# Six moves in a fused strided-attention and MLP kernel: a load, a memset, the order of a sum, two matmuls, four attention pieces and a store

## The chip, the cores and the metric

The kernel runs on one core of a Trainium2 chip. The metric is the device time of one execution in microseconds (us), as the median of several runs. Beside it stands one execution that was recorded by the hardware profiler; its rows give start and duration of each instruction, counted from the start of the recorded span.

## The reference

There are 8 batches of 8 heads, with 576 positions and a head dimension of 64. Heads 0 to 3 attend to the last 32 positions, heads 4 to 7 to all earlier positions with the same remainder modulo 32. The attention's output, 4608 tokens of 512 numbers, goes through a two-layer MLP with a PReLU between the layers.

```python
mask_local = (rel >= 0) & (rel < stride)
mask_strided = (rel >= 0) & (pos[None, :] % stride == pos[:, None] % stride)
masks = np.stack([mask_local if h < H // 2 else mask_strided for h in range(H)], axis=0)
scores = np.where(masks[None, :, :, :], scores, -1000000000.0)
...
attn = attn / (np.sum(attn, axis=-1, keepdims=True) + 1e-09)
...
h = x @ w_in
g = np.maximum(h, 0.0) + alpha * np.minimum(h, 0.0)
return (g @ w_out).astype(np.float32)
```

Inputs and outputs are float32; the kernel works in float16 with float32 accumulation. w_in is 512x2048, w_out 2048x512.

## The kernel before

**Attention** goes by pairs of heads. Pair g belongs to batch g // 4; the first two pairs of a batch are local (6 blocks of 96 queries against 128 keys), the last two strided (8 residues with 72 queries and keys). For each pair there are pieces: T turns q or k of the local heads by TensorE, S (`score_both`, or `sc1` in the part written by hand) computes scores, exponentiates them on ScalarE (ACT) and multiplies them by a mask on GpSimd (POOL) or VectorE (DVE), P (`pv_piece`) multiplies by v and divides by the sum of the row, which is a reciprocal (L437) and a multiplication (L439) on DVE, and X turns the result into `xT`, the MLP's input with tokens along the free axis. From batch 2 on, most turns are DMA transposes on SyncE's (SP's) queue: `x_dma` for the result, `transpose_d` for the strided q and k. These are first loaded row by row into `qsd` and `ksd` by `load_d(b)`, two DMAs on POOL's queue; there is one such buffer for each of q and k, so a batch's load waits until the transposes of the batch before have read it. P28.1 means the second P piece of pair 28.

**The MLP** goes by 9 chunks of 512 tokens. The first layer of chunk n is 16 pieces (`lin1_piece(n, m)`), each with four 128x512 matmuls over kk, the four pairs of heads in `xT` (L613). Each writes a PSUM bank `hps`, of which there are three. ACT makes `neg`, the negated negative part (L621), and DVE joins both to `gT` (L624) and frees the bank. The second layer of chunk 0 is plain: `U(kf)` (L884) does three token tiles and `W(i)` (L899) two matmuls of the fourth, with kf = 2i and 2i + 1. From chunk 1 on the second layer is a 2x2x2 product with seven multiplications in place of eight (`lin2_fast`, steps "1" to "7"), which needs sums of the weights (`wsum`, made once) and of the activations (`gsum`, L653, made for each chunk on POOL and DVE). A step stores its 256x256 block by `store` (L664 on DVE where something is added, L662 on ACT otherwise), followed by a DMA on SP's queue.

**Order.** Every instruction is wrapped in `keep`, so each engine runs its instructions in the order in which the program emits them. The start and chunk 0's second layer are lists written by hand. For chunks 1 to 8 there is a loop of 30 steps: step i is a first-layer piece for i < 16 and a part of the second layer after that, and behind each step a number of attention pieces (`cnt`) is emitted. For most chunks that number comes from a running sum, half as fast in the first 16 steps as later; chunk 6 has a list of steps of its own. `late` holds functions that are called at the start of the next `attn_step`; with `cnt` at 0, `attn_n` still calls `attn_step` once, which empties the list.

```python
for nm in "qk":
    keep(nc.vector.memset(qks[nm][64:80], 0.0))
keep(nc.vector.memset(x16s[64:80], 0.0))
keep(nc.vector.tensor_copy(id32, ident[0:72, 0:72]))
...
keep(nc.gpsimd.memset(vss[0][:, :, :, 64:65], 1.0))
...
load_v(0, True)
load_v(0, False)
for c in range(4):
    load_w(c, False)
```

`x16s` is the result buffer of the strided pairs from batch 2 on; its rows 72 to 79 are padding that the DMA transposes read. `load_v(0, True)` loads `stv` (the strided v), `load_v(0, False)` loads `vl` (the local v), `load_w` the parts of w_in; all are on POOL's queue.

Of the kernel before, what the change touches and what calls it, by code (L numbers as in the profile page):

```python
# [9 lines left out]
F32 = mybir.dt.float32  # L10
F16 = mybir.dt.float16
ALU = mybir.AluOpType
# [20 lines left out]
def kernel(  # L33
# [10 lines left out]
    nc = tc.nc  # L44
# [421 lines left out]
    def x_dma(P):  # L466
        if P.strided:
            P.xs = xpool.tile([128, 8, 80], F16, tag="xs", bufs=2, name="xs")
            keep(nc.sync.dma_start_transpose(P.xs, P.x16[0:80, :]))
        else:  # L470
            for s0, d0, w in spans(P.b):
                keep(nc.sync.dma_start_transpose(
                    xT[:, P.hp, d0 : d0 + w].rearrange("r (w p) -> r w p", p=96),
                    P.x16[0:96, 128 * (s0 // 96) : 128 * ((s0 + w) // 96)]))
# [14 lines left out]
    def T(u, nm):  # L489
        return lambda: transpose_piece(u, nm)  # L490
# [10 lines left out]
    for g in range(7, npair + 2):  # L501
        c = g // 4
        a, p, t = g, g - 1, g + 1
        okA = 8 <= a < npair
        okP = 8 <= p < npair
        okT = 8 <= t < npair and t < 4 * NX and (t % 4 == 0 or t < 4 * DX and t % 2 == 0)
        nP = len(pairs[p].pgroups) if okP else 0
        seq = []
        if okA:
            seq.append(("S", lambda a=a: score_both(pairs[a])))  # L510
        if okP:
            seq.append(("P", Pv(p, 0)))
        if okT:
            seq.append(("T", T(t // 2, "q")))
        if 8 <= g - 2 < npair and not pairs[g - 2].xd:
            seq.append(("X", X(g - 2)))
        if okP:
            seq.append(("P", Pv(p, 1)))
        if okT:
            seq.append(("Tk", T(t // 2, "k")))  # L520
        if nP == 3:
            seq.append(("P", Pv(p, 2)))
        if g == 14:
            seq[0], seq[1] = seq[1], seq[0]
        if not seq:
            seq.append(("N", lambda: None))

        todo = [(c, pr) for pr in range(2)] if g % 4 == 0 and 8 < g < npair else []

        if g % 4 == 1 and 9 <= g and c + 1 < B:  # L530
            todo = [(c + 1, nm) for nm in "qk"]
        lastP = max([i for i, z in enumerate(seq) if z[0] == "P"], default=len(seq) - 1)
        nslots = [i for i, z in enumerate(seq) if z[0][0] != "S"] or list(range(len(seq)))
        for i, (kind, fn) in enumerate(seq):
            extra = []
            if todo and i in nslots:
                left = len([z for z in nslots if z >= i])
                cnt = -(-len(todo) // max(1, left))
                extra = [todo.pop(0) for _ in range(min(cnt, len(todo)))]

            def run(fn=fn, extra=extra, g=g, c=c, kind=kind, lastp=(i == lastP), first=(i == 0),
                    second=(i == min(1, len(seq) - 1))):
                fn()
                for b, pr in extra:
                    if pr in ("q", "k"):
                        if b == 3:
                            continue
                        if b < NX:
                            cast_l(b, pr)
                        if b + 1 < NX:  # L550
                            load_qk(b + 1, pr)
                        continue
                    if b == 3:
                        continue
                    cast_v(b, pr, "pool")
                    if pr == 1 and b + 1 < B:
                        load_v(b + 1, True)
                if first and g % 4 == 2 and NX <= c + 1 < B:
                    turn_rows(c + 1)
                if lastp and g % 4 == 3 and NX <= c + 2 < B:  # L560
                    load_rows(c + 2, "k")
                if lastp:
                    if 4 * DX <= g - 1 < npair and pairs[g - 1].xd:
                        x_dma(pairs[g - 1])
                    if g % 4 == 3 and DX < c + 1 < B:
                        transpose_d()
                    if g % 4 == 2 and DX < c and c + 1 < B:
                        load_d(c + 1)
                    if g % 4 == 1 and DX < c and c + 1 < B:
                        load_v(c + 1, False)  # L570
                    if g % 4 == 1 and NX <= c + 2 < B:
                        load_rows(c + 2, "q")
                if second and 4 * DX <= g - 3 < npair and pairs[g - 3].xd and pairs[g - 3].strided:
                    after.append(lambda: x_copy(pairs[g - 3]))
            feed(run, g - 2 if kind == "X" else -1)
# [25 lines left out]
    def lin1_piece(n, m, begin=False):  # L601
        if n not in gTs:
            gTs[n] = gpool.tile([128, 16, 512], F16, tag="gT", name="gT")
        c0 = (512 * n) % RING
        hps = begun.pop(m, None)
        if hps is None:
            pool, tag = (pspool, "ps") if n == 0 and m // 3 % 2 else (phpool, "hps")
            hps = pool.tile([128, 512], F32, tag=tag, name="hps")
            order = (0, 1, 2, 3) if n else (2, 3, 0, 1)
        else:  # L610
            order = (0, 1)
        for kk in order[0:2] if begin else order:
            keep(nc.tensor.matmul(  # L613
                hps, win16[:, kk, 128 * m : 128 * m + 128], xT[:, kk, c0 : c0 + 512],
                start=(kk == (0 if n else 2)), stop=(kk == (3 if n else 1))))
        if begin:
            begun[m] = hps
            return

        neg = npool.tile([128, 512], F32, tag="neg", name="neg")  # L620
        keep(nc.scalar.activation(neg, hps, AF.Relu, scale=-1.0))  # L621

        def fin():
            keep(nc.vector.scalar_tensor_tensor(  # L624
                gTs[n][:, m, :], neg, oma[:, m : m + 1], hps, op0=ALU.mult, op1=ALU.add))
        late.append(fin)
# [43 lines left out]
    bank = {}  # L670

    def lin2_fast(n, i):
# [58 lines left out]
        if x == "1":  # L731
            bank["b"] = phpool.tile([128, 512], F32, tag="hps", name="ops")
            keep(nc.scalar.copy(bank["b"], bank["a"]))
        elif x in "56":
            z = npool.tile([128, 512], F32, tag="par", bufs=2, name="par")
            keep(nc.scalar.copy(z, bank[b]))  # L736
            bank["s" + x] = z
        elif x == "2":
            store(n, 0, 0, bank["a"])
        elif x == "7":  # L740
            late.append(lambda: store(n, 1, 1, bank["b"], bank["s5"]))
        elif x == "3":
            late.append(lambda: store(n, 0, 1, bank["e"], bank["s6"]))
        else:
            store(n, 1, 0, bank["b"])
# [40 lines left out]
    keep(nc.vector.memset(kTs[0][:, :, 608:672], 0.0))  # L786
    for nm in "qk":
        keep(nc.vector.memset(qks[nm][64:80], 0.0))
    keep(nc.vector.memset(x16s[64:80], 0.0))
    keep(nc.vector.tensor_copy(id32, ident[0:72, 0:72]))  # L790

    keep(nc.gpsimd.memset(vss[0][:, :, :, 64:65], 1.0))
# [30 lines left out]
    def ov(b, eng, c0, c1):  # L823
        return lambda: over_v(b, eng, c0, c1)
# [82 lines left out]
    def ws(z):  # L907
        return lambda: wout_sum(z, "dve", 0)

    def sc1(g, eng="dve"):  # L910
        return lambda: score_both(pairs[g], eng)

    for fn in [
        vs(1, 0, "pool"), sc1(6), U(0), vs(1, 1, "pool"), U(1), sc1(7), U(2), U(3), Cl(1, "q", "act"), Pv(6, 1),
        Cl(1, "k"), Pv(6, 2), Pv(6, 0), U(4), U(5), Pv(7, 0), Pv(7, 1), U(6), loads2, T(2, "q"), U(7), Pv(7, 2), W(0), W(1),
        T(2, "k"), ws(0), ws(1), ws(2), W(2), sc1(4), U(8), W(3), ov(1, "dve", 0, 24), U(9), sc1(5, "pool"), W(4), U(10), X(7, "act"), U(11),
        X(6, "act"), Pv(4, 1), W(5), Cl(2, "q", "act"), Cl(2, "k", "act"), U(12), Pv(4, 0), U(13), Pv(5, 0), U(14), Pv(5, 1),
        U(15), W(6), X(4, "dve"), X(5, "dve"), W(7)]:
        fn()
# [18 lines left out]
    for n in range(1, NCH):  # L938
# [3 lines left out]
        for i in range(30):  # L942
# [5 lines left out]
            if n == 1 and i == 15:  # L948
                held.extend(late)
                late.clear()  # L950
            if n == 6:
                cnt = int(i in (2, 5, 7, 9, 16, 17, 19, 20, 22, 24, 25, 27))
            elif n == 1:
                cnt = int(i > 12 or i in (0, 2, 4, 6, 9, 11))
            else:
                acc += left / (19.5 if n == B - 2 else 21) * (0.5 if i < 16 else 1.0)
                cnt = int(acc)
                acc -= cnt
# [14 lines left out]
                load_v(3, True)  # L973
            if i == 15:
                load_v(3, False)
                load_d(3)
                cast_l(3, "q", "act")
            if i == 17:
                cast_l(3, "k", "act")
# [35 lines left out]
```

## Time and profile before

| | |
|---|---|
| median of 3 runs | 297.91 us (297.36 to 298.34) |
| profiled execution, its own time | 296.76 us |
| its span | 294.9 us |
| granted TensorE clock | 1.0 |
| PE busy | 289.3 us |
| DVE, ACT, POOL busy | 216.1, 182.1, 181.7 us |
| DMA engines | busy for most of the first 28 of 40 slices, little after |

The span is what the recorded instructions cover; the rest of the profiled execution's time lies around it. Busy time of PE counts matmuls in flight, so a high share says that PE is rarely without work, not that it works at its peak. PE, PEld (the weight loads beside it), DVE, ACT, POOL and SP are the engines; an "issue" in place of a releaser means that the profile shows nothing that the engine waited for.

### The profile page before, as it was taken

The numbers are of one execution on the slowest core, as the hardware profiler recorded it, in microseconds if no ns is written. First come the engines' busy times: TensorE is split into PE (matmuls) and PEld (weight loads), VectorE is DVE, ScalarE is ACT, GpSimd is POOL, SyncE is SP. The second block draws the span as 40 slices with busy tenths as digits, with TensorE's granted clock in tenths as the row PEclk, the third lists the DMA queues.
The fourth block names the chain that finished last, engine by engine and source line by source line (L and its number), as shares of the span: only waits on it lengthen the run. The fifth ranks groups of instructions, "written<-read, shape, count | busy, mean of one in ns | idle before, by whom it ended". The sixth has DMA issues, their size and how long they took to land.

```text
span 294.9 us, 6948 instructions
## 1 busy us (share of the span) xinstructions
PE 289.3 (98%) x2732; PEld 187.3 (64%) x2732; DVE 216.1 (73%) x412; ACT 182.1 (62%) x337; POOL 181.7 (62%) x167
## 2 busy tenths in 40 slices
PE   8999999999999999999999999999999999999995
PEld 3764554545885488547864786478646864784584
DVE  5688876579966895689668975897489948927851
ACT  1777756797957864775477537754776266417630
POOL 8462547999589997889897985777364105002200
PEclk9999999999999999999999999999999999999999
DMA  7999999999999999999999999976411230021004
GB/s 180 263 194 203 239 212 258 221 158 336 114 110 196 153 151 129 195 136 153 174 185 146 122 144 194 134 115 117 150 20 23 58 109 0 0 87 58 2 0 143
DMA packets 97488, 41.18 MB, mean 140 GB/s; under 512 B 75360, under 2 KB 94256, under 8 KB 97456
## 3 DMA queue, kind: packets, MB, share of 16 engines
q0 software_dynamic: 51008, 17.77, 59.7%
q1 hardware_dynamic: 46096, 22.32, 37.2%
q10 hardware_dynamic: 352, 0.66, 0.9%
q8 instruction: 21, 0.34, 0.5%
q14 instruction: 11, 0.09, 0.1%
HBM read 38.24 MB, written 9.44 MB: 162 GB/s over the span
## 4 chain that ended last, share of the span: by engine, by line
PE 91%; DVE 3%; DMA 2%; issue 2%; ACT 1%; SPq 0%; DVEq 0%; ACTq 0%
PE hps L613 41%; PE ops L719 22%; PE ops L709 8%; PE pv L430 5%; PE ops L884 4%; PE sp L377 2%; DMA consts<-consts 2%; PE tp L292 1%; PE xp L455 1%; PE sph L377 1%; PE ops L899 1%; DVE gT L624 1%; PE tf L154 1%; DVE gsum L653 1%; PE wps L761 1%
## 5 line engine op out<-in xcount | busy, mean ns | idle before, releaser
L613 PE MATMUL hps<-xT,win 128*128 128x512 f16 x576 | 132.9, 379 | 0.1
L624 DVE SCALAR_TENSOR_TENSOR gT<-neg,oma,hps 128x512 f16<-128x512 f32 x144 | 105.2, 744 | 36.2 <-ACT neg L621 28.6
L621 ACT ACTIVATE neg<-hps 128x512 f32<-128x512 f32 x144 | 85.8, 598 | 34.6 <-PE hps L613 32.4
L613 PEld LDWEIGHTS <-win 128*128 128x128 f16 x576 | 53.3, 98 | 58.3 <-issue 0.8
L653 POOL TENSOR_TENSOR gsum<-gT 128x1024 f16<-128x1024 f16 x15 | 31.8, 2123 | 37.6 <-DVE gT L624 37.5
L402 POOL TENSOR_TENSOR et<-et,consts 128x576 f16<-128x576 f16 (+1 forms) x23 | 32.1, 1394 | 34.7 <-ACT et L400 34.4
L719 PEld LDWEIGHTS <-gT 128*128 128x128 f16 x384 | 35.7, 98 | 6.1 <-issue 0.5
L439 DVE TENSOR_TENSOR x<-pv,rc 96x384 f16<-96x384 f32 (+2 forms) x62 | 33.0, 532 | 2.1
L719 PE MATMUL ops<-wout,gT 128*128 128x256 f16 x256 | 32.1, 273 | 0.0
L709 PE MATMUL ops<-wsum,gsum 128*128 128x256 f16 x248 | 30.7, 273 | 0.2 <-DVE gsum L653 0.2
L409 POOL TENSOR_TENSOR et<-et,consts 128x576 f16<-128x576 f16 (+1 forms) x23 | 29.7, 1290 | 0.1
L430 PEld LDWEIGHTS <-et 72*128 72x128 f16 (+1 forms) x448 | 23.6, 98 | 8.4 <-ACT et L339 0.4
L709 PEld LDWEIGHTS <-gsum 128*128 128x128 f16 x256 | 23.6, 98 | 3.3 <-DVE gsum L653 0.4
L719 PEld LDWEIGHTS <-gsum 128*128 128x128 f16 x256 | 23.7, 98 | 2.9
L400 ACT ACTIVATE et<-sp 128x576 f16<-128x576 f32 (+1 forms) x24 | 15.5, 645 | 16.4 <-PE sp L377 16.4
L664 DVE TENSOR_TENSOR osb<-ops,par 128x512 f32<-128x512 f32 (+1 forms) x16 | 10.7, 674 | 17.1 <-PE ops L719 9.4
L437 DVE RECIPROCAL rc<-pv 72x6 f32<-72x6 f32 (+2 forms) x80 | 14.7, 183 | 10.2 <-PE pv L430 9.8
L662 ACT COPY osb<-ops 128x512 f32<-128x512 f32 x16 | 9.4, 587 | 16.8 <-PE ops L719 16.7
L406 ACT ACTIVATE et<-sph 128x288 f16<-128x288 f32 (+1 forms) x48 | 18.9, 409 | 0.0
L736 ACT COPY par<-ops 128x512 f32<-128x512 f32 x15 | 8.8, 587 | 13.1 <-PE ops L709 12.6
L719 PE MATMUL ops<-wsum,gT 128*128 128x256 f16 x128 | 16.1, 273 | 0.3 <-DVE osb L664 0.3
L719 PE MATMUL ops<-wsum,gsum 128*128 128x256 f16 x128 | 16.1, 272 | 0.0
(112 smaller groups left out, 354.5 us busy)
## 6 DMA issues: line engine op xcount, KB each, us to landing
out_dram<-osb SPq DMA_DIRECT2D x35, 256.0 KB, 3.0
vl<-in_v_dram POOLq DMA_DIRECT2D x6, 384.0 KB, 9.7
win<-in_moe_w_in_dram POOLq DMA_DIRECT2D x4, 512.0 KB, 17.4
wout<-in_moe_w_out_dram POOLq DMA_DIRECT2D x4, 512.0 KB, 17.1
qsd<-in_q_dram POOLq DMA_DIRECT2D x7, 288.0 KB, 7.5
ksd<-in_k_dram POOLq DMA_DIRECT2D x7, 288.0 KB, 8.8
stv<-in_v_dram POOLq DMA_DIRECT2D x7, 288.0 KB, 7.7
ql<-in_q_dram SPq DMA_DIRECT2D x3, 576.0 KB, 8.8
```

The costliest lines, as they stand in the source:

```text
L400: keep(nc.scalar.activation(ev.rearrange("r (y c) -> r y c", y=2), sp[0:r, :, 0:n], AF.Exp, scale=SCALE))
L402: keep(mul(mv, mv, m, op=ALU.mult))
L406: keep(nc.scalar.activation(ev[:, n * y : n * y + n], sps[y][0:r, 0:n], AF.Exp, scale=SCALE))
L409: keep(mul(mv, mv, m, op=ALU.mult))
L430: keep(nc.tensor.matmul(pv[:, 65 * x : 65 * x + 65], et[0:r, c : c + 128], v16[0:r, 2 * P.pr + hh, t, :] if P.strided else v16[:, 6 * (2 * ...
L439: keep(nc.vector.tensor_tensor(P.x16[0:w, c0 : c0 + 64 * nb].rearrange("r (c e) -> r c e", e=64), pvv[:, :, 0:64], rc[0:w, 0:nb].unsqueeze ...
L613: keep(nc.tensor.matmul(hps, win16[:, kk, 128 * m : 128 * m + 128], xT[:, kk, c0 : c0 + 512], start=(kk == (0 if n else 2)), stop=(kk == ( ...
L621: keep(nc.scalar.activation(neg, hps, AF.Relu, scale=-1.0))
L624: keep(nc.vector.scalar_tensor_tensor(gTs[n][:, m, :], neg, oma[:, m : m + 1], hps, op0=ALU.mult, op1=ALU.add))
L653: keep((nc.vector if eng == "dve" else nc.gpsimd).tensor_tensor(gsum[i][:, hs], a, b, op=op))
L709: keep(nc.tensor.matmul(o, gsum[i][:, y, 128 * z : 128 * z + 128], wsum[i][:, y, :], start=(x == "5" and y == 0 and (z == 0 or alone)), st ...
L719: keep(nc.tensor.matmul(o, lhs(y), rhs(y), start=(first and y == 0), stop=(y == 7), skip_group_check=True))
```

## The change

There are six edits. `load_d(3)` leaves step 15 of chunk 1 and stands in the piece after which `x_dma(pairs[10])` is emitted. The memset of `x16s` goes from DVE to POOL. In chunk 1, the first layer runs over kk in the order 2, 3, 0, 1, as chunk 0 does. In chunk 0's second layer, `W(3)` goes ahead of the scores of pair 4 and `U(8)`. Chunk 6 loses its own list of steps and follows the running sum. In the last chunk, step "7" adds in two halves and stores at once, not by `late`.

```diff
                     if 4 * DX <= g - 1 < npair and pairs[g - 1].xd:
                         x_dma(pairs[g - 1])
+                    if g == 11:
+                        load_d(3)
                     if g % 4 == 3 and DX < c + 1 < B:
                         transpose_d()
...
-            order = (0, 1, 2, 3) if n else (2, 3, 0, 1)
+            order = (0, 1, 2, 3) if n > 1 else (2, 3, 0, 1)
...
-                start=(kk == (0 if n else 2)), stop=(kk == (3 if n else 1))))
+                start=(kk == (0 if n > 1 else 2)), stop=(kk == (3 if n > 1 else 1))))
...
+        elif x == "7" and last:
+            osb = opool.tile([128, 512], F32, tag="osb", name="osb")
+            for z in range(2):
+                c = slice(256 * z, 256 * z + 256)
+                keep(nc.vector.tensor_tensor(osb[:, c], bank["b"][:, c], bank["s5"][:, c], op=ALU.add))
+            keep(nc.sync.dma_start(
+                out[512 * n + 256 : 512 * n + 512, 256:512].rearrange("(r p) c -> p r c", p=128),
+                osb.rearrange("p (r c) -> p r c", r=2)))
         elif x == "7":
             late.append(lambda: store(n, 1, 1, bank["b"], bank["s5"]))
...
-    keep(nc.vector.memset(x16s[64:80], 0.0))
+    keep(nc.gpsimd.memset(x16s[64:80], 0.0))
...
-        T(2, "k"), ws(0), ws(1), ws(2), W(2), sc1(4), U(8), W(3), ov(1, "dve", 0, 24), U(9), sc1(5, "pool"), W(4), U(10), X(7, "act"), U(11),
+        T(2, "k"), ws(0), ws(1), ws(2), W(2), W(3), sc1(4), U(8), ov(1, "dve", 0, 24), U(9), sc1(5, "pool"), W(4), U(10), X(7, "act"), U(11),
...
-            if n == 6:
-                cnt = int(i in (2, 5, 7, 9, 16, 17, 19, 20, 22, 24, 25, 27))
-            elif n == 1:
+            if n == 1:
                 cnt = int(i > 12 or i in (0, 2, 4, 6, 9, 11))
             else:
                 acc += left / (19.5 if n == B - 2 else 21) * (0.5 if i < 16 else 1.0)
...
             if i == 15:
                 load_v(3, False)
-                load_d(3)
                 cast_l(3, "q", "act")
```

## The prediction, made before the changed kernel had run

> **What bounds the kernel now.** I read the page's busy times first, then its chain, then the timeline in the five stretches that the diff touches.
>
> ```profile
> PE 289.3 (98%) x2732; PEld 187.3 (64%) x2732; DVE 216.1 (73%) x412; ACT 182.1 (62%) x337; POOL 181.7 (62%) x167
> PE 91%; DVE 3%; DMA 2%; issue 2%; ACT 1%; SPq 0%; DVEq 0%; ACTq 0%
> ```
>
> PE is busy for 98% of the span and carries 91% of the chain, at full granted clock. A 128x512 matmul costs 0.216 us (the chain's stretch at 239.20: 13.81 us for 64). No edit adds or removes a matmul, so only PE's few waits can move. These are the ones near the edits, from the timeline (start, duration, engine, line, operation; in brackets the idle time before it and who ended it):
>
> ```profile
> 1.41 1.55 POOL L212 DMA_DIRECT2D stv<-in_v_dram  x2 [0.25 <-issue]
> 4.49 0.48 DVE L789 MEMSET x16s<- 16x512 uint32 x1
> 6.89 0.19 DVE L790 CAST id<-consts 72x72 f32<-72x72 f16 x1 [1.92 <-DMA consts<-consts]
> 10.12 0.43 DVE L232 COPY vs<-stv 72x1024 f16<-72x1024 f16 x1 [0.32 <-DMA stv<-in_v_dram]
> 11.20 0.35 PE L430 MATMUL pv<-vs,et 72*128 72x65 f16 x6
> ...
> 44.39 0.59 PE L899 MATMUL ops<-wout,gT 128*128 128x512 f16 x2
> 44.59 0.72 DVE L232 COPY kT<-tp 128x512 f16<-128x512 f16 x1 [0.73 <-PE tp L292]
> 45.46 0.30 PE L377 MATMUL sp<-qT,kT 64*128 64x96 f16 x6 [0.47 <-DVE kT L232]
> 46.48 0.59 PE L899 MATMUL ops<-wout,gT 128*128 128x512 f16 x2
> ...
> 220.83 0.55 DVE L439 TENSOR_TENSOR x<-pv,rc 96x384 f16<-96x384 f32 x1
> 221.30 2.20 DVE L624 SCALAR_TENSOR_TENSOR gT<-neg,oma,hps 128x512 f16<-128x512 f32 x3
> 222.09 2.25 PEld L613 LDWEIGHTS <-win 128*128 128x128 f16 x11 [0.40 <-issue]
> 226.90 1.76 DVE L653 TENSOR_TENSOR gsum<-gsum,gT 128x1024 f16<-128x1024 f16 x1
> 230.41 1.05 PE L709 MATMUL ops<-wsum,gsum 128*128 128x256 f16 x8 [0.23 <-DVE gsum L653]
> ...
> 288.23 1.02 DVE L664 TENSOR_TENSOR osb<-ops,par 128x512 f32<-128x512 f32 x2 [4.03 <-issue]
> 288.98 1.91 PE L719 MATMUL ops<-wsum,gT 128*128 128x256 f16 x16 [0.32 <-DVE osb L664]
> ```
>
> Read each group as: what arrives last before PE goes on. At 10.12 it is the strided v (stv); at 45.46 the copy of batch 1's k; at 222.09 a DVE that is behind; at 230.41 a DVE sum; at 288.98 a DVE store.
>
> **The named edit, load_d(3): nothing.** In the program it moves from step 15 of chunk 1 into the piece P10.2 at step 21. The order of instructions on each engine shows what that does. On POOL's queue the two loads stand where they stood, between the load of vl and the mask of pair 12's scores, because between steps 15 and 21 POOL is given nothing (pair 11's masks are DVE's, and the q and k casts go to ACT). Both wait for the same semaphores at the same values. On SP nothing moves: its transposes of pair 10's x, then of qsd and ksd, keep their order and waits. An identical queue has an identical cost, 0.
>
> **Memset of x16s, from DVE to POOL: +0.2.** DVE is freed of the 0.48 at 4.49, but it then idles 1.92 for the constants, so that gains nothing. On POOL it becomes the first instruction, ahead of every POOL load, and the memset of vs behind it now waits for its end. It writes 1024 f16 elements per row. The nearest rows bound its time: POOL's memset of 32x64 took 0.22, its copies of 72x1024 f16 at 33.08 took 2.02 for two. I take 1.0, from the row with the same count. [...]
>
> So the issues of stv, vl and win slip by about 1.0. If stv lands 1.0 later, DVE's copy ends at 11.55, the first PV matmul starts at about 11.65 in place of 11.20, and DVE's cast of qT, which stands behind that copy and opens the scores of pair 3, ends near 12.0 in place of 11.11: PE resumes at 12.05 in place of 11.47, 0.6 late. PE, ACT and DVE then follow each other up to chunk 0, so the 0.6 stays. The cover is queueing. The two 144 KB stv loads land 8.7 after issue, later ones of 288 KB in 7.7 (median), with the DMA engines at 7 and 9 tenths in the first slices: part of the 8.7 is not the issue's. A third of 0.6 is my value, 0.2; the ends are -0.3 (stv earlier by DVE's 0.32 of idle time) and +1.05 (below).
>
> **W(3) ahead of sc1(4): -0.43.** W(2)'s second matmul has handed over at 44.39 + 2 x 0.216 = 44.82; PE then waits until 45.46, 0.64. W(3)'s two matmuls (those at 46.48) need only gT 6 and 7 and wout, both long there: 2 x 0.216 = 0.43 of the wait is filled. Scores 4 still start at 45.46, and U(9) and all behind it come 0.43 sooner. What could be late next: scores 5 at 47.65 would come at 47.22, with their two PSUM banks free when the exps at 46.34 (0.71) end, at 47.05. PV 4 at 50.27 needs masks that end at 47.95. Covered. The whole wait would be -0.64, half the fill -0.2.
>
> **Order of kk in chunk 1: 0.** The first piece reads pairs 6 and 7 first, so X(4) and X(5) have 0.43 more. The weight load there waited 0.35 for DVE, but PE only 0.03 behind W(7). It guards the 0.43 of the edit before, whose DVE work at this place may not come earlier in full.
>
> **Chunk 6's spread: -0.28.** The formula gives the steps 3, 6, 9, 12 in place of 2, 5, 7, 9; the eight from 16 on stay. A lin1 piece costs PE 0.863 and DVE 0.66 back to back; a PV adds 0.19 to PE and 0.69 to DVE. Before, P29.0 and P29.1 stand two pieces apart, DVE gains 2 x 0.20 between them and falls behind: gT of step 10 ends at 222.04, and the matmul of step 13, which needs its bank, starts at 222.09 instead of 221.81: 0.28. With steps 9 and 12, counted from the chunk's first matmul: step 13 can start at 12.25 and gT 10 ends at 12.23, a tie; gT 12 ends at 13.65 before step 15 at 13.97; gT 15 starts when its neg is there. So PE reaches step 16 0.28 sooner, DVE too. POOL's first sum now stands ahead of pair 30's mask and starts at about 5.1, since its four gT are done; pair 30's masks then end by 10.2, PV 30 wants them after 15. The wait of 0.23 at 230.41 comes from DVE's sum of 1.76 (others 0.69) beside POOL's mask of pair 31, which keeps its step, so it stays. Ends: -0.5 (that wait goes as well) and +0.2 (the tie is lost, or the sums start late).
>
> **Last chunk's "7": +0.07.** The store leaves `late`, but that list was emptied right after the same step, so its place is the same. What changes is one add of 512 (0.69) into two of 256, each 0.42 (row at 291.85); they overlap by 0.08, as the two adds at 288.23 do: 0.34 + 0.42 = 0.76. Only the second half signals, and the matmul at 288.98 waits for that: +0.07, straight to the end. Ends 0 and +0.1.
>
> **Sum:** 0 + 0.2 - 0.43 + 0 - 0.28 + 0.07 = -0.44. The profiled execution took 296.76 (span 294.9, 1.9 around it), which is 1.15 under the median of the runs, 297.91. It becomes 296.3; the median 297.5.
>
> **The rivals.**
>
> *POOL's loads come sooner.* [...] Chance 0.3, with both of its sizes.
>
> *The memset holds win too (slower).* The first part of win is waited for by POOL's wout issue at 19.71, the first lin1 matmul is at 19.64: no slack. If the slip of 1.0 reaches win whole, PE stands at that matmul, 1.05 late: 1.05 - 0.43 - 0.28 + 0.07 = +0.41, 298.3. It decides above a slip of 0.64. Against it: win lands 15 to 21 after issue, with the DMA engines full, and full engines make up a late issue. Chance 0.15.
>
> *Chunk 6 loses.* PV 29 at step 12 is nearer to the sums at 16. If DVE enters them late, +0.2 for -0.28: +0.04, 298.0; no change. Chance 0.1.
>
> **From cases to numbers.** The forecast has 0.45. A measurement here tells some 0.3%, 0.9 us (the three runs lie 0.98 apart). Over 0.9 faster: most of the first rival and a part of the forecast's spread, 0.36; slower by that: a part of the second rival with an unfavourable draw of runs, 0.15; between, 0.49. The range takes the first rival's larger size (296.6) and the second's end (298.3) with a little of the runs' scatter: 296.5 to 298.5.
>
> **What would show it.** Right: POOL's first load near 2.4 and stv's copy on DVE at 10.1 to 10.5; four L899 matmuls in a row ahead of scores 4; no gap at step 13 of chunk 6; two adds of 0.42 near 288; POOL's qsd and ksd loads at their old place. Wrong: the first lin1 matmul a whole microsecond late, a wait at 45 as long as before, or a wait for DVE sums in chunk 6 above 0.4.

## The result, and the profile after

The changed kernel takes 296.51 us (median of 21 runs, 295.54 to 301.99); the kernel before, beside it, 297.36 (21 runs, 296.45 to 298.87). The ratio is 0.9966 (95% interval 0.9955 to 0.9977): 1.0 us less, between 0.7 and 1.3 (the two medians lie 0.85 apart). The prediction had 0.44 less.

The profiled execution of the changed kernel is not a typical one: 297.44 us with a span of 295.6, so 0.7 longer than the profiled execution of before (296.76), though the median is shorter. What follows is therefore read stretch by stretch. First two lines of its page: the busy times, and the shares of the chain that ended last.

```profile
PE 289.3 (98%) x2732; PEld 187.5 (63%) x2732; DVE 215.7 (73%) x412; ACT 182.2 (62%) x337; POOL 183.4 (62%) x168
PE 67%; DMA 21%; DVE 4%; POOL 2%; ACT 2%; issue 2%; SPq 0%; POOLq 0%; DVEq 0%; ACTq 0%
```

PE's work is the same 289.3 us. But in this execution the chain runs through DMAs for 21% of the span (2% before): loads landed late. The timeline of the changed kernel at the five places shown of before, and at a sixth (88 to 91 us); start, duration, engine, line, operation, and in brackets the idle time before it and who ended it:

```profile
0.73 0.94 POOL L799 MEMSET x16s<- 16x1024 f16 x1 [0.29 <-POOLq L1006]
1.95 1.56 POOL L212 DMA_DIRECT2D stv<-in_v_dram  x2
10.51 0.43 DVE L232 COPY vs<-stv 72x1024 f16<-72x1024 f16 x1 [0.66 <-DMA stv<-in_v_dram]
11.24 0.35 PE L430 MATMUL pv<-vs,et 72*128 72x65 f16 x6
...
44.43 1.03 PE L909 MATMUL ops<-wout,gT 128*128 128x512 f16 x4
45.51 0.30 PE L377 MATMUL sp<-qT,kT 64*128 64x96 f16 x6
...
54.20 1.15 ACT L230 CAST kl<-kl 128x1152 f16<-128x1152 f32 x1 [1.13 <-DMA kl<-in_k_dram]
55.26 1.07 ACT L230 COPY osb<-ops 128x512 f32<-128x512 f32 x2
55.89 1.02 PE L615 MATMUL hps<-xT,win 128*128 128x512 f16 x4 [0.50 <-ACT osb L230]
...
89.03 1.40 ACT L478 COPY xT<-xs 128x384 f16<-128x384 f16 x2 [1.30 <-DMA xs<-x16s]
90.85 2.10 PE L615 MATMUL hps<-xT,win 128*128 128x512 f16 x9 [0.46 <-ACT xT L230]
...
223.18 2.75 PE L615 MATMUL hps<-xT,win 128*128 128x512 f16 x12
224.74 0.55 DVE L439 TENSOR_TENSOR x<-pv,rc 96x384 f16<-96x384 f32 x1
225.21 2.21 DVE L626 SCALAR_TENSOR_TENSOR gT<-neg,oma,hps 128x512 f16<-128x512 f32 x3
226.00 1.03 PE L721 MATMUL ops<-wout,gT 128*128 128x256 f16 x8
226.00 0.75 PEld L721 LDWEIGHTS <-gT 128*128 128x128 f16 x7 [0.34 <-issue]
228.06 0.69 DVE L655 TENSOR_TENSOR gsum<-gsum,gT 128x1024 f16<-128x1024 f16 x1
228.09 1.79 POOL L402 TENSOR_TENSOR et<-et,consts 72x576 f16<-72x576 f16 x1 [4.90 <-ACT et L400]
228.40 1.91 PE L711 MATMUL ops<-wsum,gsum 128*128 128x256 f16 x16
230.33 1.04 PE L711 MATMUL ops<-wsum,gsum 128*128 128x256 f16 x8
...
288.80 0.81 DVE L746 TENSOR_TENSOR osb<-ops,par 128x256 f32<-128x256 f32 x2 [3.68 <-issue]
289.61 0.42 DVE L666 TENSOR_TENSOR osb<-ops,par 128x256 f32<-128x256 f32 x1
289.66 1.91 PE L721 MATMUL ops<-wsum,gT 128*128 128x256 f16 x16
```

What to see: POOL's memset takes 0.94 and its first load is issued at 1.95 (before 1.41), and DVE's copy of stv starts at 10.51 (before 10.12), when stv lands; the first PV matmul is 0.04 later than before. Four matmuls stand ahead of scores 4. At 55.89 PE waits for ScalarE, which had waited for k. At 89.03 ScalarE waits 1.30 for pair 10's turned x, and PE for ScalarE. In chunk 6 no wait is left at step 13, but one of 0.34 for the weights (0.23 for PE) has come up at 226.00, where the second layer begins. The row names no releaser, but the semaphores of the trace do: step 16 writes the PSUM bank of step 13, which DVE frees with the gT of step 13, the first of the three at 225.21. DVE makes it after the PV of step 12 (224.74) and signals its end at 225.96, and PE goes on 0.04 later. The DVE sum that took 1.76 beside POOL's mask now takes 0.69, and the matmuls at 228.40 and 230.33 follow without a wait. At 288.80 the first half of the add comes 3.68 after DVE's last work; before, it was 4.03.

The runs scatter, so I cut each profile into stretches between the first matmuls of its parts. The same stretch has the same length in all kernels unless something in it differs. The runs of e1 to e4, e5 to e8, e9 to e12 and e13 to e16 were taken on four chips, each with the kernel before beside them (medians 297.34, 297.33, 297.31 and 297.47), so compare ratios, not medians. In us:

| kernel | first PV to first lin1 | layer 2 of chunk 0, to chunk 1 | chunk 1 | chunk 2 | chunk 6 | chunk 8 to last matmul | median | ratio to before (95%) |
|---|---|---|---|---|---|---|---|---|
| before | 8.44 | 19.64 | 33.38 | 30.94 | 29.49 | 26.41 | 297.36 | |
| after | 8.44 | 20.05 | 33.61 | 31.63 | 29.03 | 26.18 | 296.51 | 0.9966 (0.9955 to 0.9977) |
| e1: store alone | 9.20 | 19.64 | 33.38 | 30.97 | 29.49 | 26.47 | 297.48 | 1.001 (0.9989 to 1.003) |
| e2: chunk 6 alone | 8.44 | 19.64 | 33.38 | 30.96 | 29.03 | 26.41 | 296.98 | 0.9992 (0.9974 to 1.0009) |
| e3: W(3) and kk alone | 8.44 | 19.19 | 33.23 | 31.42 | 29.49 | 26.43 | 296.77 | 0.9989 (0.997 to 1.0008) |
| e4: named load alone | 8.45 | 19.64 | 33.38 | 31.31 | 29.48 | 26.41 | 297.53 | 1.0001 (0.9983 to 1.0019) |
| e5: memset alone | 8.44 | 19.64 | 33.38 | 30.96 | 29.49 | 26.06 | 296.91 | 0.9977 (0.9956 to 0.9999) |
| e6: after without memset | 8.87 | 19.19 | 33.24 | 32.11 | 29.03 | 26.47 | 296.8 | 0.9981 (0.996 to 1.0002) |
| e7: after without store | 8.44 | 19.67 | 33.23 | 30.98 | 29.03 | 26.05 | 295.9 | 0.9944 (0.9926 to 0.9962) |
| e8: after again | 8.44 | 19.19 | 33.64 | 32.64 | 29.03 | 26.19 | 296.7 | 0.9971 (0.995 to 0.9992) |
| e9: e7, load behind | 8.44 | 19.19 | 33.23 | 31.44 | 29.03 | 26.05 | 296.34 | 0.9968 (0.9957 to 0.998) |
| e10: load behind alone | 8.74 | 19.97 | 33.73 | 31.44 | 29.49 | 26.43 | 297.55 | 1.001 (0.9998 to 1.0022) |
| e11: W(3) alone | 8.70 | 19.21 | 33.38 | 30.93 | 29.49 | 26.41 | 296.94 | 1.0 (0.9982 to 1.0019) |
| e12: e7 again | 8.45 | 19.23 | 33.48 | 33.06 | 29.03 | 26.06 | 296.77 | 0.9979 (0.9957 to 1.0001) |
| e13: memset split | 8.44 | 19.64 | 33.38 | 30.94 | 29.49 | 26.05 | 297.23 | 0.9989 (0.9971 to 1.0006) |
| e14: e7, casts on DVE | 8.44 | 19.19 | 33.81 | 31.82 | 29.03 | 26.05 | 296.29 | 0.997 (0.9944 to 0.9996) |
| e15: e9, casts on DVE | 8.44 | 19.40 | 34.60 | 30.93 | 29.03 | 26.05 | 297.46 | 0.9991 (0.9977 to 1.0005) |
| e16: e9 again | 9.69 | 19.18 | 33.23 | 31.41 | 29.03 | 26.05 | 296.51 | 0.9967 (0.9953 to 0.9982) |

Three lengths vary by execution. The first holds a wait of PE for the first part of win in e1, e6, e10 and e11, and in e16 a granted clock of 0.55 from 12.5 to 16.3 us. Ahead of chunk 1, 19.40 to 20.05 (19.97 in e10, with the old order) holds a wait for ScalarE's late cast of kl, as at 54.20 above. In chunk 1, 33.48 to 33.81 holds one for batch 2's transposed strided k, ahead of the scores of pair 10, worth 0.25 to 0.58 (0.30 of e15's 34.60 is the same). e10 has these last two without any edit of the change ahead of them. But they stand in three and five of the eight profiles with the memset, chunk 6, W(3) and kk edits together, and in one each of the other ten; whether the edits make them more frequent is open. The stretches that are left out agree in all: chunk 0's first layer 16.1 to 16.2, chunks 3 to 5 29.93 each, chunk 7 26.04. The length of a stretch shows an edit of 0.1 us; the time of a run, which differs by 1 us and more between executions, seldom does. The ratios leave out a few executions that ran disturbed (301.99 above is one).

### The profile page after: what moved, and what is told of

It reads as the page before. It is cut to its first block, busy times and chain, and to the rows that moved or that the text cites. A ratio compares the mean times of both kernels' runs of the same rounds, so it can differ in the third digit from the quotient of the medians.

```text
span 295.6 us, 6949 instructions
## 1 busy us (share of the span) xinstructions
PE 289.3 (98%) x2732; PEld 187.5 (63%) x2732; DVE 215.7 (73%) x412; ACT 182.2 (62%) x337; POOL 183.4 (62%) x168
## 4 chain that ended last, share of the span: by engine, by line
PE 67%; DMA 21%; DVE 4%; POOL 2%; ACT 2%; issue 2%; SPq 0%; POOLq 0%; DVEq 0%; ACTq 0%
PE hps L615 33%; PE ops L721 20%; DMA kl<-in_k_dram 9%; PE ops L711 8%; DMA win<-in_moe_w_in_dram 6%; DMA kT<-ksd 3%; PE pv L430 3%; DMA xs<-x16s 2%; PE sp L377 2%; DVE gsum L655 1%; DVE gT L626 1%; PE sph L377 1%; PE tp L292 1%; ACT neg L623 1%; POOL vl L222 1%
## 5 line engine op out<-in xcount | busy, mean ns | idle before, releaser
L666 DVE TENSOR_TENSOR osb<-ops,par 128x512 f32<-128x512 f32 (+1 forms) x15 | 10.1, 674 | 13.1 <-PE ops L721 9.4
L721 PE MATMUL ops<-wsum,gT 128*128 128x256 f16 x128 | 16.1, 273 | 0.1
L721 PE MATMUL ops<-wsum,gsum 128*128 128x256 f16 x128 | 16.2, 272 | 0.0
```

The lines of the kernel that those rows point to most:

```text
L721: keep(nc.tensor.matmul(o, lhs(y), rhs(y), start=(first and y == 0), stop=(y == 7), skip_group_check=True))
```

## The experiments

### One edit at a time, on the kernel before

**e1, the store of step 7** (the change's block ahead of the old branch):

```diff
+        elif x == "7" and last:
+            osb = opool.tile([128, 512], F32, tag="osb", name="osb")
...
         elif x == "7":
```

> Only the last chunk's step 7 is changed (two adds of 256, stored at once). Theory of the prediction: +0.07 us, because only the second half signals and the two adds take 0.76 in place of 0.69. Theory after the result: the stretch from chunk 8's first matmul to the last matmul is 26.18 us in place of 26.41, since DVE starts the first half 0.37 us after step 7's last matmul begins, where the whole add started 0.71 after it; then -0.23 here too. Rival: the 0.71 was an accident of that one execution (DVE fetched late); then this profile shows the stretch anywhere from 26.1 to 26.5 and the time is unchanged within its interval.

Measured: 26.47 in place of 26.41, +0.06; nothing else differs but a late start (9.20), which the edit cannot reach.

**e2, chunk 6's spread:**

```diff
-            if n == 6:
-                cnt = int(i in (2, 5, 7, 9, 16, 17, 19, 20, 22, 24, 25, 27))
-            elif n == 1:
+            if n == 1:
```

> Only chunk 6 follows the running sum. Theory of the prediction: the stretch from chunk 6's to chunk 7's first matmul falls by 0.28 us from 29.49, since the wait for DVE's sum beside POOL's mask of pair 31 stays. Theory after the result: it falls by 0.46 to 29.03, because the sum now ends before that mask begins, as in the profile of the changed kernel; the time falls by 0.3 to 0.5 us. Rival: only the 0.28 is systematic and the rest depends on which of the two starts first, in each execution anew.

Measured: 29.03 in place of 29.49, -0.46, and the same in every kernel with this edit. From the starts of PE's matmuls: the wait of 0.28 at step 13 went, 0.23 came up at step 16 (for DVE's gT of step 13, as shown above), and the 0.40 that PE lost behind the DVE sum went whole: -0.45. The mask of POOL beside that sum stood in the profile of before as

```profile
226.78 1.34 POOL L402 TENSOR_TENSOR et<-et,consts 72x576 f16<-72x576 f16 x1 [3.74 <-ACT et L400]
```

**e3, W(3) ahead of scores 4 with the order of kk; e11, W(3) without it:**

```diff
-... W(2), sc1(4), U(8), W(3), ov(1, "dve", 0, 24), ...
+... W(2), W(3), sc1(4), U(8), ov(1, "dve", 0, 24), ...
-            order = (0, 1, 2, 3) if n else (2, 3, 0, 1)
+            order = (0, 1, 2, 3) if n > 1 else (2, 3, 0, 1)
```

> W(3) ahead of the scores of pair 4, and chunk 1's kk order. Theory: the stretch from chunk 0's first second-layer matmul to chunk 1's first matmul falls by 0.43 us from 19.64 to 19.2, and the time by as much, wherever the casts on ACT are not late. Rival, from the profile of the changed kernel: ACT's cast of batch 2's k waits for its load and stands ahead of the two copies that free PSUM banks, so the gain is lost in executions where that load lands late (20.05 there); then the time falls by 0.1 to 0.3 on the median.

> Only W(3) ahead of scores 4, with the order of kk in chunk 1 as before. It separates the two edits that ran together so far. My reading: the stretch from chunk 0's second layer to chunk 1's first matmul becomes 19.2 us (19.64 before), and chunk 1 to chunk 2 stays at 33.38, as the first lin1 piece still waits some 0.15 us in its middle for X(5). The rival: the 0.15 us belong to the order of pieces, and chunk 1 to chunk 2 is 33.23 here too, so that the order of kk is worth nothing, as predicted. Time about 0.45 us below that of the kernel before, unless chunk 2 gives it back (to 31.5 us).

Measured: the stretch ahead of chunk 1 is 19.19 and 19.21 (before 19.64), so W(3) alone brings -0.43 to -0.45. Chunk 1 is 33.23 with both and 33.38 with W(3) alone, so the order of kk brings -0.15. PE's weight loads at the first lin1 piece of chunk 1, in the timeline of e11:

```profile
55.18 0.11 PEld L613 LDWEIGHTS <-win 128*128 128x128 f16 x2 [0.36 <-DVE xT L232]
55.54 0.31 PEld L613 LDWEIGHTS <-win 128*128 128x128 f16 x2 [0.25 <-issue]
```

And in that of e3:

```profile
54.91 0.74 PEld L613 LDWEIGHTS <-win 128*128 128x128 f16 x4
```

Without the edit the weights come in two pairs, with 0.36 ahead of them and 0.25 between them; PE hides all but 0.15 of that. With it the four stream.

**e4, the named edit**, with which batch 3's strided q and k are loaded from the piece behind `x_dma(pairs[10])`:

```diff
+                    if g == 11:
+                        load_d(3)
...
-                load_d(3)
```

> Only the named edit: load_d(3) emitted behind the turning of pair 10's x. Theory: no engine's queue changes, so the time is that of before within its interval, and the differences of this profile to that of before (the stretches up to chunk 3 above all, where loads land) are what one execution differs from another. Rival: the time falls by up to 0.5 us, the part of the measured -1.0 that the prediction's sum lacks.

Measured: nothing. Every stretch is that of before but chunk 2 (31.31), where the turned x landed 0.98 late; that comes and goes without the edit (below). The two loads are issued at 76 us, five us ahead of the transposes of pair 10's x, in the changed kernel too: in the instruction stream they are not behind the turning.

**e5, the memset of x16s on POOL:**

```diff
-    keep(nc.vector.memset(x16s[64:80], 0.0))
+    keep(nc.gpsimd.memset(x16s[64:80], 0.0))
```

> Only the memset goes from DVE to POOL. Prediction: +0.2 us at the start (ends -0.3 and +1.05). From the profiles so far: from the first PV matmul to the first first-layer matmul 8.44 us as before, so 0 at the start. New theory for the end: DVE's instruction number 447 starts 0.35 late because it has to be fetched; before, it is the last chunk's step-7 add, for which PE waits, and one instruction fewer ahead of it makes that add number 446. Then the add starts 0.37 us after step 7's last matmul in place of 0.72, and the stretch from chunk 8 to the last matmul is 26.06 in place of 26.41. Rival: the short lag of the changed kernel comes from the halving of the add together with other edits; then 26.41 stays.

Measured: from the first PV matmul to the first lin1 matmul it is 8.44, unchanged. That stretch begins only after stv has landed, and stv lands later with this edit: 10.79 on average over the nine profiles with the memset on POOL, 10.14 over the nine without. The first PV matmul starts at 11.58 and 11.39 on average, the first lin1 matmul (without e16 and its low clock) at 19.99 and 20.02, with medians of 20.02 and 19.91. These starts scatter by 0.6 to 0.8, so a cost of 0.1 to 0.2 at the start is neither shown nor excluded. The last stretch, however, is 26.06, -0.35, 280 us after the edit. The add of step 7 in this kernel's timeline:

```profile
288.33 1.24 DVE L664 TENSOR_TENSOR osb<-ops,par 128x512 f32<-128x512 f32 x2 [3.68 <-issue]
```

Before, it came 4.03 after DVE's work ended, here 3.68. Relative to the last matmul of step 7 it starts 0.37 after that one began instead of 0.72.

### The changed kernel, with one edit taken back

**e6: after, with the memset on VectorE. e7: after, without the block of step 7. e8: after itself.**

> The changed kernel with the memset back on DVE. Theory of the fetch: the first half of the step-7 add is number 447 again, starts 0.72 late, and the stretch from chunk 8 to the last matmul is 26.47 (26.18 with the memset on POOL): 0.3 us slower than the changed kernel. Rival: 26.18 stays.

> The changed kernel with the last chunk's step 7 as before (one add of 512, by the list late). Theory of the fetch: the add is number 446 and starts 0.37 late, takes 0.69: the stretch from chunk 8 to the last matmul is 26.06, 0.12 us better than with two halves. So the store edit costs 0.1 and the memset gains 0.35 at the other end of the kernel. Rival: the store edit carries the gain; then 26.4 and a loss of 0.2.

> The changed kernel once more, on the same chip as the three beside it, for a second profile. Theory: the stretches that hold no load (chunk 6 at 29.03, chunk 8 to the end at 26.18) are as in its first profile; those up to chunk 3 are shorter where the loads land in time: about 19.2 from chunk 0's second layer to chunk 1 in place of 20.05, and 30.9 to 31.4 in chunk 2. The time is 0.9 to 1.1 us below before. Rival: the late loads belong to the change (POOL issues later), and 20.05 stays.

Measured: the last stretch is 26.47 without the memset's move, 26.05 without the store, 26.19 with both. So the memset brings -0.28 to -0.35 there, and the store costs 0.06 alone but 0.13 beside the memset. e7 was the fastest of all (295.9, in 6 runs), e8 had 296.7. In chunk 2 of e6 and e8 ScalarE waited 1.79 and 2.32 for the turned x; in e7 it waited for nothing. A second run of e7 had it too:

> The changed kernel without its edit of step 7 once more, as the fastest so far: by the stretches -0.45, -0.15, -0.46 and -0.35, -1.4 us in all where nothing lands late: median 295.9 to 296.2, chunk 8 to the last matmul 26.05 us.

Measured: 296.77; the edits' stretches are as expected (26.06, 29.03, 19.23), but chunk 2 took 33.06. From its timeline:

```profile
90.12 1.40 ACT L478 COPY xT<-xs 128x384 f16<-128x384 f16 x2 [2.73 <-DMA xs<-x16s]
```

So e7's 295.9 had luck in it: its interval lies below 1 and e12's reaches it, and whether this kernel beats the changed one the times do not tell. By the stretches they should, by 0.13.

### Why the memset acts at the end

In the kernel before, the add of step 7 is number 447 of VectorE's records in the trace (counted from 0, its waits on semaphores too). With the memset gone from VectorE it is number 446. Two kernels move the number the other way: e13 leaves VectorE's work as it was, e14 gives it two copies more.

**e13: the kernel before, VectorE's memset in two halves** (add becomes 448). **e14: e7 with the two casts of batch 3's strided v on VectorE** (448; it also has `load_d(3)` at its old place, the edit that e4 shows to change nothing).

```diff
-    keep(nc.vector.memset(x16s[64:80], 0.0))
+    for z in range(2):
+        keep(nc.vector.memset(x16s[64:80, 512 * z : 512 * z + 512], 0.0))
```

```diff
-                    cast_v(3, pr, "pool")
+                    cast_v(3, pr, "dve")
```

> The kernel before, with VectorE's memset of x16s split into two of half the columns: the same work on the same engine, and one instruction more on VectorE, 4 us in. Theory 1 (VectorE's instruction number 447 has to be fetched, whatever it is, and starts some 0.35 us late): the add of step 7 in the last chunk becomes number 448 and starts 0.37 us after step 7's last matmul began instead of 0.72; chunk 8 to the last matmul 26.05 us instead of 26.41, the time 0.35 us shorter, for an instruction more. Theory 2 (the memset on VectorE, or its sharing of memory with GpSimd, is what costs at the end): 26.41, no change. Theory 3 (every instruction from 447 on is late): 26.41.

> The changed kernel without its edit of step 7, and with the two casts of batch 3's strided v at 84 us (2.02 us on GpSimd) on VectorE, which does such a copy in 0.43. VectorE has two instructions more, so the add of step 7 is number 448 again. Theory 1 of the fetch at number 447: chunk 8 to the last matmul stays 26.05 us; theory 3 (all from 447 on): 26.41. In chunk 2 the loads stay where they are: if the turned x lands late by their transfers, chunk 2 to 3 still goes from 30.9 to 33 us by execution, median 295.9 to 296.8.

Measured: 26.05 in both. e13, timeline:

```profile
288.58 1.24 DVE L664 TENSOR_TENSOR osb<-ops,par 128x512 f32<-128x512 f32 x2 [3.67 <-issue]
```

An instruction *more* on VectorE gives the same 0.35 us as one less. So neither the memset's engine nor its work is the cause, and not everything from 447 on is late: the lag is at that one place in the stream. The add starts 0.72 to 0.74 after the matmul in all eight profiles where it is number 447 (before, e1 to e4, e6, e10, e11), and 0.36 to 0.37 in all ten where it is 446 (after, e5, e7 to e9, e12, e16) or 448 (e13 to e15). Where the add is 446 and 447 is the wait behind it (e5, e7, e9, e12, e16), it is this 447 that comes late, 0.39 behind the add; a wait that follows the add as 448 or 449 comes 0.04 to 0.08 behind. There PE does not wait for it, as the add itself still runs. The lag is no wait for an operand: in the profile of before PE's signal for the add comes at 287.80 and ScalarE's at 286.67, VectorE's wait for PE ends at 287.84, and the add starts at 288.23; in e5 that wait ends at 288.29 and the add starts at 288.33. The time of e13 alone (ratio 0.9989, interval across 1) could not have told.

That it is a fetch of instructions is my reading. The trace has something for it: among its DMA packets are some of a kind `instruction`, and the last one of queue 14 (8192 bytes) starts 0.65 to 0.71 us after record 447 in 14 of the 15 profiles where the add is 446 or 447 (0.94 in the other, that of after). In the three where it is 448 that packet starts 15.7 us ahead of the add. So such a packet stands at that place and moves with the number. But it starts after the late record, so that the record waits for a fetch is not shown.

### What chunk 2 gives back

**e9, e16: e7 with the two loads truly behind the turning. e10: the same on the kernel before.** Their transposes go with them (the diff is that of e10; in e9 and e16 the `load_d(3)` that goes is the one behind `if g == 11`):

```diff
-                    if g % 4 == 3 and DX < c + 1 < B:
+                    if g % 4 == 3 and g != 11 and DX < c + 1 < B:
                         transpose_d()
...
                 fn()
+                if g == 12 and first:
+                    load_d(3)
+                    transpose_d()
...
-                load_d(3)
```

> The changed kernel without its edit of step 7, and with the load of batch 3's strided q and k (and its two DMA transposes on SyncE) put truly behind the turning of pair 10's x: on GpSimd's queue its two issues now stand behind the mask of the scores of pair 12's first half, and its transposes behind those of pair 10's x. Theory 1 (the wait of chunk 2 for the turned x comes from these two loads, whose transfers run beside the two small transposes): from the issue of the transposes to the copy of xT on ScalarE about 5.5 us, no wait of PE for that copy, chunk 1 to 2 first matmuls 33.2 us, chunk 2 to 3 30.9 us, median 295.8. Theory 2 (the loads have no part in it; with 0.6 us taken out of PE's path ahead, the turning is simply asked for sooner, and its landing scatters by execution): 5.5 to 8 us as before, chunk 2 to 3 between 30.9 and 32.6 us, median 295.9 to 296.7. Rival to both: the strided loads now land too late for scores 14, some 96 us in, and PE waits there by up to 2 us.

> The kernel before with this one move alone: the load and the transposes of batch 3's strided q and k truly behind the turning of pair 10's x. In the profile of before the copy of the turned x waited for nothing, so theory 1 and theory 2 both give 0 +- 0.3 us here: chunk 2 to 3 30.9 us. If the move alone costs, by more than 0.5 us, then the loads come too late for scores 14, and the place of before is the better one.

> The kernel of the load truly behind the turning once more, for the spread of its runs. Theory 1: the turned x lands in time in each, so chunk 2 to 3 is 31.44 again and no run is more than 1.2 us above the fastest; median 296.2 to 296.4. Theory 2: a third of the runs lies more than 1.2 us above the fastest, as in the changed kernel.

Measured: no wait for the turned x in any of the three, and chunk 2 31.44, 31.44 and 31.41. From the timeline of e9:

```profile
81.26 1.20 SPq L469 DMA_TRANSPOSE xs<-x16s  x1
83.18 0.79 POOL L135 DMA_DIRECT2D qsd<-in_q_dram  x1
86.81 1.41 ACT L478 COPY xT<-xs 128x384 f16<-128x384 f16 x2
```

The load now follows the transposes, and the copy comes 5.55 after them without a bracket. But 0.5 is lost at 107 to 110 us, where DVE's sums meet POOL's masks (the mask at 107.07 takes 1.74, in e7 1.29; the sum at 106.13 takes 1.54 and the two from 108.29 on 1.67, in e7 1.38 and 1.28): POOL's queue runs 1.1 late, behind the two issues of 0.79 and 0.71. e10 shows that 0.5 as well.

**e15: e9 with the two casts on VectorE**, to give POOL its time back (diff as in e14).

> The same with the load of batch 3's strided q and k truly behind the turning of pair 10's x. Without the casts, GpSimd's queue behind the two loads runs some 0.5 us ahead of the changed kernel's instead of 1.1 us behind it. Theory 1 (the load's transfers make the turned x late, and its issues the 0.5 us lost at 107 us): no wait for the turned x, chunk 2 to 3 30.9 us in place of 31.44, median 295.7 to 295.9 with no run more than 1.2 us above the fastest. Theory 2 (the load has no part in the late landing): runs up to 3 us above the fastest, as with the load in its place. Rival: the two copies hold up VectorE's store of chunk 1 or pair 11's x, and PE waits at 86 to 88 us by up to 0.8 us.

Measured: chunk 2 is 30.93, as theory 1 had it, but the rival came true as well, at a higher price than it gave: chunk 1 is 34.60. From its timeline:

```profile
84.74 2.14 DVE L232 COPY vs<-stv 72x1024 f16<-72x1024 f16 x2
85.22 1.37 POOL L409 TENSOR_TENSOR et<-et,consts 128x576 f16<-128x576 f16 x1
88.12 0.34 PE L430 MATMUL pv<-vl,et 128*128 128x65 f16 x6 [0.91 <-PE ops L722]
```

The two copies took 2.14 beside POOL's mask (0.98 in e14, where a mask of POOL was at its end as they began), the store and pair 11's x came late behind them, and PE lost 1.07 by the starts of its matmuls.

Taken together: with the load in its place, ScalarE waited 0.98 us or more for the turned x in 7 of 14 profiled executions, with it behind in 0 of 4. Of the runs, 43 of 152 lay more than 1.2 above the fastest of their kernel, against 2 of 43; the larger of those two is the profiled execution of e16, which lost its time at the start (9.69 for 8.44, with the low clock). That speaks for the load's transfers as the cause; four profiles do not prove it, and other transfers of those microseconds have not been taken away.

## Why the prediction was right or wrong

The change gains, as forecast, and three terms came out as priced: the named load, W(3) and the store alone. The size was off by 0.6. The step that failed most was the memset's: "DVE is freed of the 0.48 at 4.49, but it then idles 1.92 for the constants, so that gains nothing" looked at the next wait on DVE alone, and the edit gained 0.35 at the kernel's end. Two further terms, chunk 6 and the order of kk, were mis-sized, and chunk 2 gives a part back. (The forecast time, 297.5, also stood on 297.91 for the kernel before, which took 297.36 beside the change.)

- **The named edit, 0:** right. e4 shows no difference that is the edit's.
- **W(3), -0.43:** right, -0.45. The next late things named there were covered; one not named comes in some executions: kl of batch 2 lands late, ScalarE's cast of it stands ahead of two copies of osb, and PE waits about 0.5 for a bank ahead of chunk 1. The profiled execution of after is one, e7's is another.
- **The last chunk's step 7, +0.07:** right alone (+0.06); beside the memset +0.13, where number 447 is the second half of the add and starts 0.39 behind the first (0.34 in e1).
- **Chunk 6, -0.28:** mis-sized, -0.46, by two steps that failed in opposite directions. "So PE reaches step 16 0.28 sooner" failed: the wait left step 13 as predicted, but 0.23 of it came back at step 16: the prediction followed gT 10, 12 and 15, and not gT 13, whose bank step 16 needs and which now stands behind the PV of step 12. And "it stays", of the wait behind the sum of 1.76, failed: that wait went, and it was worth 0.40 of PE's time, not the 0.23 in its row's bracket. The reason given was that POOL's mask keeps its step. It does; but before, the mask started 0.12 ahead of the sum (226.78) and ran 1.34 while the sum took 1.76, and after, the sum starts 0.03 ahead of the mask, and it is the mask that takes longer, 1.79. The end of -0.5 held this case.
- **Order of kk, 0:** mis-sized, -0.15. The trace of before shows DVE ending 0.35 of idle time in the weight loads; I read the piece's start, where PE lost only 0.03, and not the gap of 0.15 ahead of its second matmul (55.80, 0.36 behind the first).
- **Memset, +0.2:** this term failed in sign. At the start the issues slipped by 0.54, not 1.0 (POOL had idled 0.25 ahead of its first load, and its next three memsets overlap: they start at 1.73, 1.79 and 1.88 and take 0.22 to 0.28 each). stv landed 0.65 later on average and the first PV matmul started 0.19 later, but the first part of win landed no later (19.57 and 19.62 on average with and without the edit), and at the first lin1 matmul no cost can be told from the scatter. So the +0.2 there is neither shown nor excluded. The gain of 0.35 at the end was in no term: the row at 288.23 with its 4.03 "issue" stood in my own fence, and I did not ask why an add that follows a matmul ended at issue. The memset itself took 0.94 on POOL for 1024 f16 elements a row, where 512 uint32 had taken 0.48 on VectorE; the value of 1.0 for it was near.

Worked again with these: -0.45 - 0.15 - 0.46 - 0.23 (memset and store together, at the end) = -1.29. Measured is -1.0, from -1.3 to -0.7. The 0.3 between is at the edge of the interval; what can fill it are the late landings ahead of chunk 1 and in chunks 1 and 2, and a cost of the memset at the start. A wait of 0.98 or more for the turned x stood in 6 of 7 profiles with W(3) and kk and the load in its place, and in 1 of the 7 others. That speaks against chance, though the two groups were made after the counts were seen; if it holds, these two edits give back in chunk 2, in some executions, what they win in chunks 0 and 1. It is not that the x is asked for sooner: the copy's turn comes 5.5 to 5.7 us after the issue of the transposes in all of them, and it is the landing that takes 6.7 to 8.4. Why the transfers meet more often there is open.

Of the rivals, "POOL's loads come sooner" came nearest by number, 296.6, but no run shows loads that come sooner: they are issued later, 1.95 for 1.41, and stv lands later, at 10.79 for 10.14 on average. So no run shows the term of -0.3 behind its chance of 0.3 and behind the lower end of the range; what the runs showed in its place is the 0.35 that the memset gains at the kernel's end. "The memset holds win too" fell: the issues of win begin later, at 5.28 for 4.73, but its first part lands no later, at 19.62 for 19.57 on average. The late win of e1, e6, e10 and e11 comes without the edit. "Chunk 6 loses" fell.

## What to carry to other kernels

Where an edit changes the number of an engine's instructions, look far behind it for waits that end at "issue" on that engine: a wait with no releaser may belong to a place in the stream and be moved by one instruction, as the 0.35 here was. Look at the semaphores first, though: the wait at 226.00 was marked "issue" as well, and they name DVE. Price an overlap of DVE and POOL by both durations, alone and beside (here 0.69 and 1.76 for the sum, 1.27 and 1.79 for the mask), and ask whether an edit changes which of the two starts first. And where runs scatter by more than the effect, compare stretches between fixed instructions of the profiles, not the times.

## What was not expected of the hardware

In this kernel's stream VectorE's record number 447 starts 0.35 us late, when the engine has been waiting ahead of it, whether it is the add at 288 us or the wait behind it; an add with number 446 or 448 is free of it. And where a sum of VectorE met a mask of GpSimd in chunk 6, the one that started ahead, by 0.12 or 0.03 us, kept its time and the other paid: mask 1.34 and sum 1.76 us one way round, sum 0.69 and mask 1.79 the other (elsewhere in the profile of before the same mask took 1.27 to 1.29).
